# A decode kernel with attention and a gated MLP: wq loaded in two pieces of 16 and 112 partitions, and three small moves at the kernel's end

## The chip, the cores and the metric

One core of a Trainium2 chip. The time is the device time of one execution in microseconds, the median of several runs; lower is better. The fast runs of one kernel lie within 0.2% of each other here. The profile is of one execution, and its own span is about 2 us shorter than the time (656.2 us for a run of 658.23).

## The reference, cut to what matters

```python
x = A_x                                            # (2, 1, 512), bf16
h = x + attention(layernorm(x), k_cache, v_cache, wq, wo)   # 32 heads of 128, 8192 cached positions
h2 = h + (relu(ln_h @ W_gate) * (ln_h @ W_up)) @ W_down     # ln_h = layernorm(h), F = 1376
```

Two rows of input meet 2 x 128 MB of key and value cache. The weights add 4 MB each for wq and wo and 4.2 MB for the MLP. All of it is read once, 281 MB in total.

## The kernel before

Each engine has its own list of instructions with explicit semaphores (a helper called `s`). SP issues the loads. VectorE multiplies keys by queries and adds them up. TensorE does the rest of the sums. The parts that matter here:

```python
wq_v = vt.rearrange("p t d -> p (t d)")[:, 0:KC * Hq * Dh].rearrange("p (c n) -> p c n", c=KC)
s.dma("sp", "dwq", lambda: sync.dma_start(
    out=wq_v, in_=A_wq.rearrange("(p c) n -> p c n", p=P)), writes=["va", "vb", "vc"])
load_k(0, 0, T // 2)          # keys, 4 MB
load_k(0, T // 2, T)
load_k(1)                     # 8 MB
# ... cut: norm of x, q from wq, then 16 rounds over groups of heads ...
```

wq goes into the buffer that later holds values. Each of the 128 partitions gets one contiguous row of 32 KB. The first value load waits until q is computed.

The end of the kernel, shortened:

```python
s.op("pe", lambda: mlp_in(0, gate_ps, 0, KC), reads=["hd", "gate"], ...)   # gate
# ... variance of h; up, whose last part waits for its own load; then the PE jumps ...
s.op("pe", lambda: y_rows(eye_of[:, 0:B], ar, first=True), ...)   # the residual rows into y
# ... VectorE jumps, then act = gate * up; ScalarE jumps, then act_t = columns of act ...
# ... y += act_t @ W_down, whose four slices have a load each (wda, wdb, wdc, wdd) ...
# ... y to SBUF, two stores (SP and ACT), GpSimd waits for both, then clears all semaphores ...
```

"Jumps" are branches. The code of PE, VectorE and ScalarE is laid out in parts that a small loop takes in turn, and each engine branches once to its last part.

The softmax here doesn't subtract the row's maximum and nothing guards it: scores larger than these inputs give would overflow.

Of the kernel before, what the change touches and what calls it, by code (L numbers as in the profile page):

```python
# [13 lines left out]
def _view(t, offset, dims):  # L14
    return bass.AP(tensor=t.tensor, offset=t.offset + offset, ap=[t.ap[0]] + list(dims))
# [89 lines left out]
def kernel(  # L105
# [13 lines left out]
    nc = tc.nc  # L119
    P = nc.NUM_PARTITIONS  # L120
    B, Sq, D = A_x.shape
    _, Hkv, Sk, Dh = A_k_cache.shape
    Hq = A_wq.shape[1] // Dh
    F = B_W_gate.shape[1]
    KC = D // P
# [39 lines left out]
    def sbuf(name, shape, dtype):  # L165
        return nc.alloc_sbuf_tensor(name, shape, dtype).ap()
# [8 lines left out]
    om = sbuf("om", (P, TG * Dh), f32)  # L175
# [10 lines left out]
    eye_of = sbuf("eye_of", (P, Q), f32)  # L186
# [20 lines left out]
    hd = sc2[0][:, P // 2:P].bitcast(bf16).rearrange("p (c k b) -> p c k b", k=NR, b=B)  # L207
    r2 = late[:, 2 * NK - 1:2 * NK]
    x_late = wl[0:B, NK * D + 4 * P:NK * D + 4 * P + D]
    act_t = late[:, 2 * NK:2 * NK + FC * B // 2].bitcast(bf16).rearrange("p (f b) -> p f b", b=B)  # L210
# [7 lines left out]
    y_ps = psum("y", (P, D // 2))  # L218
    sm_ps = psum("sm", (P, 512))

    s = Streams(nc, ("pe", "dve", "act", "pool", "sp"))
    for name in ("v_in", "v_two", "p_in", "p_two", "o_in", "half", "q0", "q1", "z_in", "z_out"):
        s.sem(name)
    pe, dve, act, pool, sync = nc.tensor, nc.vector, nc.scalar, nc.gpsimd, nc.sync
# [4 lines left out]
    for name, value in (("v_two", 16 * (NLOOP - 1)), ("p_two", NLOOP), ("o_in", 1), ("q0", 1),  # L229
# [6 lines left out]
        out=ident, in_=ident, compare_op=ALU.not_equal, fill=1.0, base=0, pattern=[[-1, P]],  # L236
# [9 lines left out]
    for h in range(G):  # L246
        q = slice(h * Q, (h + 1) * Q)
        s.op("pool", lambda q=q: pool.tensor_copy(eye_of[q], ident[q, q]), reads=["ident"],
             writes=["eye"])
# [29 lines left out]
    def load_k(n, lo=0, hi=T):  # L279
        t = kt[n % 2]  # L280
        keys = [f"k{n % 2}{x}" for x in parts(lo, hi)]
        s.dma("sp", f"dk{n}_{lo}", lambda: sync.dma_start(
            out=t[:, lo:hi, :], in_=rows_of(A_k_cache, n)[:, lo:hi, :]), writes=keys)

    def load_v(n, lo=0, hi=T):
# [5 lines left out]
    wq_v = vt.rearrange("p t d -> p (t d)")[:, 0:KC * Hq * Dh].rearrange("p (c n) -> p c n", c=KC)  # L291
    s.dma("act", "dx", lambda: act.dma_start(out=x_row, in_=A_x.rearrange("b s d -> (b s) d")),
          writes=["x_row"])
    s.dma("sp", "dwq", lambda: sync.dma_start(  # L294
        out=wq_v, in_=A_wq.rearrange("(p c) n -> p c n", p=P)), writes=["va", "vb", "vc"])
    load_k(0, 0, T // 2)
    load_k(0, T // 2, T)
    load_k(1)
# [4 lines left out]
         reads=["eps"], writes=["warm"])  # L303
# [9 lines left out]
    def columns_of_x():  # L313
        for c in range(KC):
# [8 lines left out]
         reads=["hs", "mean"], writes=["st"])  # L323
    s.op("dve", lambda: dve.tensor_tensor(
        out=xd, in0=xc, in1=mu_ps.unsqueeze(1).to_broadcast([P, KC, B]), op=ALU.subtract),
        reads=["xc", "st"], writes=["xd"])
    s.op("pool", lambda: pool.tensor_tensor(out=sq, in0=xd, in1=xd, op=ALU.mult), reads=["xd"],
         writes=["sq"])
    reduce_c(sq, ["sq"])
    s.op("pe", lambda: pe.matmul(out=var_ps, lhsT=mean_f, rhs=hs, start=True, stop=True),  # L330
         reads=["hs", "mean"], writes=["st"])
    s.op("act", lambda: act.activation(out=rstd, in_=var_ps, func=ACT.Sqrt, bias=eps_t, scale=1.0),
         reads=["st", "eps"], writes=["rstd"])
    s.op("dve", lambda: dve.reciprocal(out=rstd, in_=rstd), reads=["rstd"], writes=["rstd"])
    s.op("pool", lambda: pool.tensor_tensor(
        out=xnb, in0=_view(xd, 0, [[B, KC], [1, B], [0, Q]]),
        in1=_view(rstd, 0, [[0, KC], [1, B], [0, Q]]), op=ALU.mult), reads=["xd", "rstd"],
        writes=["xnb"])
    s.op("act", lambda: act.activation(out=warm, in_=xnb[0:1, 0, 0, 0:1], func=ACT.Exp),
         reads=["xnb"], writes=["warm"])  # L340
# [21 lines left out]
    for r in range(NR2):  # L362
        i, h = divmod(r, G)
        for b in range(B):
# [4 lines left out]
            if b and r < NR2 - 1:  # L369
                s.op("act", fn, writes=[key], extra=extra, gives=(f"q{r % 2}", 1),  # L370
                     token=("act", s.count["act"] + 1))
# [148 lines left out]
    for k, lo, hi in WO:  # L520
        r0 = k * NS * G * Dh
        s.dma("sp", f"dwo{k}_{lo}", lambda k=k, lo=lo, hi=hi, r0=r0: sync.dma_start(
            out=wo_sb[:, k * JG + lo:k * JG + hi, :].rearrange("p k n -> p (k n)"),
            in_=A_wo[r0:r0 + NS * G * Dh, :].rearrange("(p j) n -> p j n", p=P)[:, lo:hi, :]
            .rearrange("p j n -> p (j n)")),
            writes=[f"wo{k}_{lo}"], extra=w_free)

    s.dma("act", "dx2", lambda: act.dma_start(out=x_late, in_=A_x.rearrange("b s d -> (b s) d")),
          writes=["x_late"], extra=w_free)
# [15 lines left out]
    for key, g, w, c0, c1 in (("gate", 0, B_W_gate, 0, KC), ("up0", 1, B_W_up, 0, KC - 1),  # L545
                              ("up1", 1, B_W_up, KC - 1, KC)):
        s.dma("sp", "d" + key, lambda g=g, w=w, c0=c0, c1=c1: sync.dma_start(  # L547
            out=wgu[:, g, c0:c1].rearrange("p c n -> p (c n)"),
            in_=w.rearrange("(p c) n -> p (c n)", c=KC)[:, c0 * F:c1 * F]),
            writes=[key], extra=x_free)  # L550
# [7 lines left out]
    def load_down(key, f0, r0, rows, r):  # L558
# [12 lines left out]
        out=zs, in0=zb.rearrange("p (g u) -> p g u", u=NS),  # L571
        in1=_view(head_blk, 0, [[0, B * NGR], [1, NS]]), op=ALU.mult), reads=["head"],
        writes=["zs"], extra=[("z_out", NGR * B)])
    red(zi, zs, AXIS.X, ["zs"], ["zi"])
    s.op("dve", lambda: dve.reciprocal(out=zi, in_=zi), reads=["zi"], writes=["zi"])
    for k in range(NGR):
        if k == NGR - 1:
            gather(B * NGR - 1)
        s.op("dve", lambda k=k: dve.tensor_tensor(
            out=oc[:, k * JG:(k + 1) * JG, :], in0=ou[:, :, k].rearrange("p b j -> p j b"),  # L580
            in1=_view(zi, k, [[0, JG], [NGR, B]]), op=ALU.mult),
            reads=[f"ou{b * NGR + k}" for b in range(B)] + ["zi"], writes=[f"oc{k}"])
# [17 lines left out]
    for k, lo, hi in WO:  # L600
# [7 lines left out]
        out=ht, in_=ar_ps.rearrange("p (q i c) -> p c q i", i=Q, c=KC)),  # L608
        reads=["mm0"], writes=["osb0", "osb1", "osb2", "osb3", "mm0"])
    ar = om  # L610
    s.op("act", lambda: act.activation(out=ar, in_=ar_ps, func=ACT.Copy), reads=["mm0"],
         writes=["om"])
# [3 lines left out]
    def columns_of_h():  # L616
        for q in range(P // Q):
# [6 lines left out]
         reads=["hs", "mean"], writes=["st"])  # L624
# [3 lines left out]
        out=hd, in0=_view(hc, 0, [[B, KC], [0, NR], [1, B]]),  # L628
        in1=_view(mu_ps, 0, [[0, KC], [0, NR], [1, B]]), op=ALU.subtract), reads=["xc", "st"],
        writes=["hd"])  # L630
    s.op("dve", lambda: dve.tensor_tensor(
        out=xd, in0=hc, in1=mu_ps.unsqueeze(1).to_broadcast([P, KC, B]), op=ALU.subtract),
        reads=["xc", "st"], writes=["xd"])
    s.op("dve", lambda: dve.tensor_tensor(out=sq, in0=xd, in1=xd, op=ALU.mult), reads=["xd"],
         writes=["sq"])
    red(ss, _view(sq, 0, [[0, FT * NR], [1, B], [B, KC]]), AXIS.X, ["sq"], ["ss"])

    def y_rows(lhsT, rhs, first=False, last=False):
        m = lhsT.shape[1]
        for c in range(2):  # L640
            end = pe.matmul(out=y_ps[c * 2 * Q:c * 2 * Q + m], lhsT=lhsT,  # L641
                            rhs=rhs[:, c * D // 2:(c + 1) * D // 2],
                            start=first, stop=last, skip_group_check=True)
        return end

    up_ps = mm_ps[1]

    def mlp_in(g, ps, c0, c1):
        for c in range(c0, c1):
            for j in range(FT):  # L650
                last = pe.matmul(out=ps[j * Q:(j + 1) * Q, 0:NM],
                                 lhsT=hd[:, c].rearrange("p a b -> p (a b)"),
                                 rhs=wgu[:, g, c, j:F:FT],
                                 start=(c == 0), stop=(c == KC - 1), skip_group_check=True)
        return last

    s.op("pe", lambda: mlp_in(0, gate_ps, 0, KC), reads=["hd", "gate"], writes=["gate_o"])
    var_col = st_ps[:, 32:33]
    s.op("pe", lambda: pe.matmul(out=var_col, lhsT=ss.rearrange("p a b -> p (a b)"), rhs=mean_c,
# [4 lines left out]
    s.op("dve", lambda: dve.tensor_scalar(  # L664
        out=gt, in0=gate_ps[:, 0:NM], scalar1=0.0, scalar2=r2, op0=ALU.max, op1=ALU.mult),
        reads=["gate_o", "r2"], writes=["osb0", "osb1", "osb2", "osb3"])
    up_mostly = s.op("pe", lambda: mlp_in(1, up_ps, 0, KC - 1), reads=["hd", "up0"],
                     writes=["mm1"])
    s.wait("pe", [s.last["up1"]])
    s.op("pe", lambda: mlp_in(1, up_ps, KC - 1, KC), reads=["hd", "up1"], writes=["mm1"])  # L670
    s.cut("pe")
    s.op("pe", lambda: y_rows(eye_of[:, 0:B], ar, first=True), reads=["eye", "om"], writes=["y"])
    s.op("dve", lambda: dve.tensor_tensor(
        out=gn.rearrange("p (q j) -> p q j", j=FT), in0=_view(gt, 2 * P, [[1, NQR], [0, FT]]),
        in1=_view(head_blk, 0, [[0, NQR], [1, FT]]), op=ALU.mult),
        reads=["osb0", "head"], writes=["gn"])
    s.wait("dve", [up_mostly])
    s.cut("dve")
    s.op("dve", lambda: dve.tensor_tensor(out=actr, in0=gt[:, 0:2 * P], in1=up_ps[:, 0:2 * P],
                                          op=ALU.mult), reads=["osb0", "mm1"], writes=["act"])  # L680
    s.op("dve", lambda: dve.tensor_tensor(
        out=actn[:, 0:FR].rearrange("p (q j) -> p q j", j=FT),
        in0=gn.rearrange("p (q j) -> p q j", j=FT), in1=_view(up_ps, 2 * P, [[1, NQR], [0, FT]]),
        op=ALU.mult), reads=["gn", "mm1"], writes=["act_n"])

    act_ps = sm_ps[:, 32:32 + FA * B].rearrange("p (f b) -> p f b", b=B)
    actn_ps = rep_ps[:, 32:32 + 3 * B].rearrange("p (f b) -> p f b", b=B)
# [8 lines left out]
    def columns_of_rest():  # L696
        for u in range(3):
# [4 lines left out]

    s.op("pe", columns_of_act, reads=["act", "ident"], writes=["sm"])
    s.op("pe", columns_of_rest, reads=["act_n", "row_b"], writes=["rep"])
    s.wait("act", [s.last["up1"]])
    s.cut("act")
    s.op("act", lambda: act.activation(out=act_t[:, 0:FA], in_=act_ps, func=ACT.Copy),
         reads=["sm"], writes=["act_t"])
    s.op("dve", lambda: dve.tensor_copy(act_t[:, FA:], actn_ps), reads=["rep"], writes=["act_l"])

    def add_y(f0, f1):
# [4 lines left out]
    for key, act_key, f0, f1 in (("wda", "act_t", 0, FT), ("wdb", "act_t", FT, FA),  # L716
                                 ("wdc", "act_l", FA, FC - 1), ("wdd", "act_l", FC - 1, FC)):
        s.op("pe", lambda f0=f0, f1=f1: add_y(f0, f1), reads=[act_key, key], writes=["y"])
    y_row = sc2[0][:, P:2 * P].bitcast(bf16)
# [1 line left out]
    s.op("dve", lambda: dve.tensor_copy(y_row[y0], y_ps[y0]), reads=["y"], writes=["y0"])  # L721
    s.op("act", lambda: act.activation(out=y_row[y1], in_=y_ps[y1], func=ACT.Copy), reads=["y"],
         writes=["y1"])
    ends = []
    for c, rows, eng, e in ((0, y0, "sp", sync), (1, y1, "act", act)):
        ends.append(s.dma(eng, f"dy{c}", lambda c=c, rows=rows, e=e: e.dma_start(
            out=out.rearrange("b s d -> (b s) d")[:, c * D // 2:(c + 1) * D // 2],
            in_=y_row[rows]), reads=[f"y{c}"]))
    sems = [h.num for h in s.sems.values()]
    s.wait("pool", ends)  # L730
    s.lists["pool"].append(((), lambda: pool.sem_clear(range(min(sems), max(sems) + 1)), None))



# [4 lines left out]

    engines = (("sp", sync), ("pool", pool), ("act", act), ("pe", pe), ("dve", dve))  # L740
    inner = nc.cur_bb
    for name, engine in engines:
        only = OrderedEngineSet([engine.engine])
        if name in s.cuts:
            nc.br(f"{name}_top", engines=only)
        else:
            s.emit(name, engine)
            nc.br("done", engines=only)
# [61 lines left out]
```

## Time and profile before

| | before |
|---|---|
| time | 658.23 us (658.0 to 658.88, 3 runs) |
| profiled span | 656.2 us |
| load queue busy, share of 16 engines | 99.3% |
| VectorE busy | 93% |
| last of wq landed | 13.39 us |
| last of W_down landed | 653.08 us |

The landings are the last of the sixteen semaphore increments that the trace has for each load of weights, keys or values.

### The profile page before, as it was taken

The numbers are of one execution on the slowest core, as the hardware profiler recorded it, in microseconds if no ns is written. First come the engines' busy times: TensorE is split into PE (matmuls) and PEld (weight loads), VectorE is DVE, ScalarE is ACT, GpSimd is POOL, SyncE is SP. The second block draws the span as 40 slices with busy tenths as digits, with TensorE's granted clock in tenths as the row PEclk, the third lists the DMA queues.
The fourth block names the chain that finished last, engine by engine and source line by source line (L and its number), as shares of the span: only waits on it lengthen the run. The fifth ranks groups of instructions, "written<-read, shape, count | busy, mean of one in ns | idle before, by whom it ended". The sixth has DMA issues, their size and how long they took to land.

```text
span 656.2 us, 3121 instructions
## 1 busy us (share of the span) xinstructions
PE 120.3 (18%) x1212; PEld 49.8 (8%) x1212; DVE 612.7 (93%) x172; ACT 63.2 (10%) x161; POOL 6.4 (1%) x27
## 2 busy tenths in 40 slices
PE   2400302103030110302003030300303030031256
PEld 1100101001010000101001010100101010010012
DVE  0699999999999999999999999999999999999973
ACT  2501001010101001010100101010010101001021
POOL 3000000000000000000000000000000000000000
PEclk9855755657565565756556575555657556565756
DMA  9999999999999999989999999989999999999997
GB/s 380 451 443 411 423 447 447 423 407 447 447 447 391 439 447 447 443 387 447 447 447 415 415 447 447 443 387 447 447 447 427 403 447 447 443 403 432 425 420 311
DMA packets 6613, 281.12 MB, mean 428 GB/s; under 512 B 744, under 2 KB 848, under 8 KB 1360
## 3 DMA queue, kind: packets, MB, share of 16 engines
q1 hardware_dynamic: 6596, 281.06, 99.3%
q8 instruction: 2, 0.03, 0.0%
q14 instruction: 3, 0.02, 0.0%
q10 hardware_dynamic: 12, 0.01, 0.0%
HBM read 281.06 MB, written 0.00 MB: 428 GB/s over the span
## 4 chain that ended last, share of the span: by engine, by line
DVE 75%; DMA 24%; issue 0%; SPq 0%; PE 0%
DVE k L386 34%; DVE k L391 33%; DMA k<-in_A_k_cache_dram 21%; DVE sc L243 4%; DMA k<-in_B_W_down_dram 3%; DVE osb L471 2%; DVE om L466 1%; SPq L547 0%; DVE ou L243 0%; SPq L559 0%; DVE rep L478 0%; PE y L641 0%; DVE sc L721 0%; SPq L294 0%; SPq L805 0%
## 5 line engine op out<-in xcount | busy, mean ns | idle before, releaser
L386 DVE TENSOR_TENSOR k<-k,qrep 128x32768 bf16<-128x32768 bf16 (+3 forms) x18 | 275.8, 15322 | 6.2 <-DMA k<-in_A_k_cache_dram 6.1
L391 DVE TENSOR_TENSOR k<-k 128x8192 bf16<-128x8192 bf16 (+4 forms) x69 | 266.9, 3868 | 2.4
L417 PE MATMUL o<-v,pm 128*32 128x512 bf16 x1024 | 93.8, 544 | 478.8 <-PEq L432 478.8
L404 ACT ACTIVATE pm<-sc 32x256 bf16<-32x256 f32 (+2 forms) x68 | 48.0, 705 | 560.1 <-DVE sc L243 559.3
L417 PEld LDWEIGHTS o<-v,pm 128*32 128x32 bf16 x1024 | 38.5, 130 | 533.5 <-issue 527.7
L243 DVE TENSOR_REDUCE sc<-k 128x256 f32<-128x2048 bf16 (+2 forms) x17 | 36.6, 2151 | 0.1
L471 DVE TENSOR_REDUCE osb<-om 128x128 f32<-128x512 f32 x16 | 16.3, 1018 | 0.6
L404 ACT ACTIVATION_READ_ACCUMULATOR pm<-sc 32x1 f32 x68 | 15.7, 231 | 0.0
L466 DVE TENSOR_TENSOR om<-o,turn_of 128x512 f32<-128x512 f32 x16 | 10.9, 682 | 3.9 <-PE o L417 3.9
L350 PE MATMUL mm<-v,om 128*64 x32 | 9.5, 432 | 6.6 <-PEq L348 6.6
L243 DVE TENSOR_REDUCE pick<-ident 128x8 f32<-128x128 bf16 x1 | 0.4, 382 | 10.7 <-ACT qrep L367 10.7
L367 ACT ACTIVATE qrep<-mm 32x512 bf16<-32x512 f32 x16 | 9.4, 587 | 6.1 <-PE mm L350 5.2
L451 PE MATMUL rep<-osb,spread 128*32 128x128 f32 x32 | 2.6, 421 | 37.1 <-DVE osb L471 37.1
L538 POOL TENSOR_TENSOR zm<-zm,zx 128x1 f32<-128x1 f32 x1 | 0.2, 192 | 625.9 <-PE o L417 625.9
L320 DVE COPY xc<-st 128x8 f32<-128x8 f32 x1 | 0.2, 167 | 6.5 <-PE st L315 6.5
L350 PEld LDWEIGHTS mm<-v,om 128*64 128x64 bf16 x32 | 3.9, 121 | 11.8 <-issue 11.0
L607 DVE STREAM_TRANSPOSE osb<-mm 128x512 f32<-128x512 f32 x1 | 0.7, 716 | 3.8 <-PE mm L593 3.8
L593 PE MATMUL mm<-k 128*2 128x512 bf16 x32 | 3.8, 621 | 0.3 <-DMA k<-in_A_wo_dram 0.3
L451 PEld LDWEIGHTS rep<-osb,spread 128*32 128x32 f32 x32 | 0.8, 140 | 37.5 <-DVE osb L471 37.5
L446 PE MATMUL sm<-zm,same 128*128 128x16 f32 x8 | 1.8, 297 | 0.4 <-PEq L432 0.4
L721 DVE CAST sc<-y 2x256 bf16<-2x256 f32 x1 | 0.4, 413 | 1.5 <-PE y L641 1.5
L240 POOL MEMSET pm<- 128x2048 bf16 x1 | 1.8, 1805 | 0.1
(81 smaller groups left out, 34.9 us busy)
## 6 DMA issues: line engine op xcount, KB each, us to landing
v<-in_A_v_cache_dram SPq DMA_DIRECT2D x4, 4096.0 KB, 20.3
k<-in_A_k_cache_dram SPq DMA_DIRECT2D x2, 4096.0 KB, 26.3
v<-in_A_wq_dram SPq DMA_DIRECT2D x1, 4096.0 KB, 12.4
k<-in_A_wo_dram SPq DMA_DIRECT2D x1, 2048.0 KB, 20.2
k<-in_A_wo_dram SPq DMA_DIRECT2D x2, 1024.0 KB, 23.2
k<-in_B_W_gate_dram SPq DMA_DIRECT2D x1, 1376.0 KB, 13.2
k<-in_B_W_up_dram SPq DMA_DIRECT2D x1, 1032.0 KB, 15.3
k<-in_B_W_down_dram SPq DMA_DIRECT2D x2, 512.0 KB, 17.0
```

The costliest lines, as they stand in the source:

```text
L240: s.op("pool", lambda: pool.memset(pm, 0.0), writes=["pm"])
L243: s.op("dve", lambda: dve.tensor_reduce(out=out_, in_=in_, axis=axis, op=ALU.add), reads=reads, writes=writes)
L350: last = pe.matmul(out=mm_ps[t][0:B * Q], lhsT=xnb[:, c].rearrange("p b q -> p (b q)"), rhs=wq_r[:, c, :, bass.ds(r * 2 + t, 1), :], start ...
L367: fn = lambda src=src, dst=dst: act.activation(out=dst, in_=src, func=ACT.Copy)
L386: s.op("dve", lambda: dve.tensor_tensor(out=kp, in0=kp, in1=_view(qrep[:, b, i, :], 0, [[0, hi - lo], [1, Dh]]), op=ALU.mult), reads=keys ...
L391: s.op("dve", lambda half=half, width=width: dve.tensor_tensor(out=kp[:, :, 0:half], in0=kp[:, :, 0:half], in1=kp[:, :, half:width], op=AL ...
L404: last = act.activation(out=p_of[ps, lo // TG:hi // TG, :, h], in_=sc2[n % 2][ps, lo:hi].rearrange("p (g t) -> p g t", t=TG), func=ACT.Exp ...
L417: last = pe.matmul(out=o_ps[g:g + W2], lhsT=pm[:, t // TG, :], rhs=vt[:, t:t + TG, :].rearrange("p t d -> p (t d)"), start=(t < P // Q * T ...
L451: last = pe.matmul(out=rep_ps[u * Q:(u + 1) * Q, :], lhsT=spread.rearrange("k h m -> k (h m)"), rhs=osb[:, u, :], start=True, stop=True, s ...
L466: s.op("dve", lambda: dve.tensor_tensor(out=om.rearrange("p (t d) -> p t d", d=Dh), in0=o_ps.rearrange("p (t d) -> p t d", d=Dh), in1=_vie ...
L471: s.op("dve", lambda: dve.tensor_reduce(out=osb[:, n % NS, :], in_=om.rearrange("p (t d) -> p d t", d=Dh), axis=AXIS.X, op=ALU.add), reads ...
L593: last = pe.matmul(out=ar_ps[g:g + B], lhsT=oc[:, k, :], rhs=wo_sb[:, k, :], start=False, stop=(k + P // Q >= NK), skip_group_check=True)
```

## The change

Its intent, as far as the code tells: get work out of the last microseconds, and get the first load going in a small piece. There are four parts.

```diff
-    s.dma("sp", "dwq", lambda: sync.dma_start(
-        out=wq_v, in_=A_wq.rearrange("(p c) n -> p c n", p=P)), writes=["va", "vb", "vc"])
+    for lo, hi in ((0, P // 8), (P // 8, P)):
+        s.op("sp", lambda lo=lo, hi=hi: sync.dma_start(
+            out=wq_v[lo:hi], in_=A_wq.rearrange("(p c) n -> p c n", p=P)[lo:hi]),
+            writes=["va", "vb", "vc"], gives=("dwq", 16), token=("dwq", 16 if lo == 0 else 32))
...
+    s.op("pe", lambda: y_rows(eye_of[:, 0:B], ar, first=True), reads=["eye", "om"], writes=["y"])
     s.op("pe", lambda: mlp_in(0, gate_ps, 0, KC), reads=["hd", "gate"], writes=["gate_o"])
...
     s.cut("pe")
-    s.op("pe", lambda: y_rows(eye_of[:, 0:B], ar, first=True), reads=["eye", "om"], writes=["y"])
...
-    s.wait("dve", [up_mostly])
-    s.cut("dve")
     s.op("dve", lambda: dve.tensor_tensor(out=actr, in0=gt[:, 0:2 * P], in1=up_ps[:, 0:2 * P],
...
+    s.wait("dve", [s.last["act"]])
+    s.cut("dve")
...
-    s.wait("act", [s.last["up1"]])
-    s.cut("act")
     s.op("act", lambda: act.activation(out=act_t[:, 0:FA], in_=act_ps, func=ACT.Copy),
          reads=["sm"], writes=["act_t"])
+    s.wait("act", [s.last["act_t"]])
+    s.cut("act")
...
-    s.wait("pool", ends)
-    s.lists["pool"].append(((), lambda: pool.sem_clear(range(min(sems), max(sems) + 1)), None))
+    s.wait("pool", [("gone", 2)])                 # both stores issued
+    s.lists["pool"].append(((), clear, None))     # all semaphores but y_out
+    s.lists["pool"].append(
+        ((), lambda: pool.wait_ge(s.sem("y_out"), 32).then_inc(s.sem("y_out"), -32), None))
```

More of the change, by code (lines that the diff above doesn't have):

```diff
@@ L219, with clear @@
     sm_ps = psum("sm", (P, 512))
-    s = Streams(nc, ("pe", "dve", "act", "pool", "sp"))
+    s = Streams(nc, ("y_out", "pe", "dve", "act", "pool", "sp"))
+    def clear():
+        sems = [h.num for k, h in s.sems.items() if k != "y_out"]
+        pool.sem_clear(range(min(sems), max(sems) + 1))
     for name in ("v_in", "v_two", "p_in", "p_two", "o_in", "half", "q0", "q1", "z_in", "z_out"):
@@ L293 @@
           writes=["x_row"])
-    s.dma("sp", "dwq", lambda: sync.dma_start(
-        out=wq_v, in_=A_wq.rearrange("(p c) n -> p c n", p=P)), writes=["va", "vb", "vc"])
+    for lo, hi in ((0, P // 8), (P // 8, P)):
+        s.op("sp", lambda lo=lo, hi=hi: sync.dma_start(
+            out=wq_v[lo:hi], in_=A_wq.rearrange("(p c) n -> p c n", p=P)[lo:hi]),
+            writes=["va", "vb", "vc"], gives=("dwq", 16), token=("dwq", 16 if lo == 0 else 32))
+        for k in ("va", "vb", "vc"):
+            token = s.last.pop(k)
+    for k in ("va", "vb", "vc"):
+        s.last[k] = token
     load_k(0, 0, T // 2)
@@ L666 @@
         reads=["gate_o", "r2"], writes=["osb0", "osb1", "osb2", "osb3"])
-    up_mostly = s.op("pe", lambda: mlp_in(1, up_ps, 0, KC - 1), reads=["hd", "up0"],
-                     writes=["mm1"])
+    s.op("pe", lambda: mlp_in(1, up_ps, 0, KC - 1), reads=["hd", "up0"], writes=["mm1"])
     s.wait("pe", [s.last["up1"]])
@@ L723 @@
          writes=["y1"])
-    ends = []
     for c, rows, eng, e in ((0, y0, "sp", sync), (1, y1, "act", act)):
-        ends.append(s.dma(eng, f"dy{c}", lambda c=c, rows=rows, e=e: e.dma_start(
+        s.op(eng, lambda c=c, rows=rows, e=e: e.dma_start(
             out=out.rearrange("b s d -> (b s) d")[:, c * D // 2:(c + 1) * D // 2],
-            in_=y_row[rows]), reads=[f"y{c}"]))
-    sems = [h.num for h in s.sems.values()]
-    s.wait("pool", ends)
-    s.lists["pool"].append(((), lambda: pool.sem_clear(range(min(sems), max(sems) + 1)), None))
+            in_=y_row[rows]), reads=[f"y{c}"], gives=("y_out", 16))
+        s.lists[eng].append(((), lambda e=e: e.sem_inc(s.sem("gone"), 1), None))
+    s.wait("pool", [("gone", 2)])
+    s.lists["pool"].append(((), clear, None))
+    s.lists["pool"].append(
+        ((), lambda: pool.wait_ge(s.sem("y_out"), 32).then_inc(s.sem("y_out"), -32), None))
     engines = (("sp", sync), ("pool", pool), ("act", act), ("pe", pe), ("dve", dve))
     inner = nc.cur_bb
+    for name in [w for ops in s.lists.values() for waits, _, gives in ops
+                 for w in [k for k, _ in waits] + ([gives[0]] if gives else [])]:
+        s.sem(name)
     for name, engine in engines:
```

## The prediction

The forecast's sum came to 659.0 us (657.0 to 665.0). It stands between rival (a), in which the split of wq costs nothing (657.9), and rival (b), in which the places that the two pieces are written to slow them (661 to 666, centred at 662.5). The chance for slower by 2% (above 671.4 us) was 0.025. The "hint" is one for (b): packets that slow each other.

> **What bounds the kernel now.** I read the page from the top: busy shares, slices, queues, chain. First the shares, the DMA row and the queue:
>
> ```profile
> span 656.2 us, 3121 instructions
> ...
> PE 120.3 (18%) x1212; PEld 49.8 (8%) x1212; DVE 612.7 (93%) x172; ACT 63.2 (10%) x161; POOL 6.4 (1%) x27
> ...
> DMA  9999999999999999989999999989999999999997
> GB/s 380 451 443 411 423 447 447 423 407 447 447 447 391 439 447 447 443 387 447 447 447 415 415 447 447 443 387 447 447 447 427 403 447 447 443 403 432 425 420 311
> ...
> q1 hardware_dynamic: 6596, 281.06, 99.3%
> ```
>
> Two resources are nearly full: VectorE at 93% and the one load queue at 99.3% of sixteen engines. The queue wins. The packet records of the trace have the first load packet at 1.97 us and the last at 652.60 us, and in each 10 us between there is at most 0.01 us without sixteen packets in flight. A 64 KB packet takes 2.42 us, so sixteen engines move 16 x 65,536 B / 2.42 us = 433 GB/s, and 281.06 MB at that rate takes 649 us. That is the span less the 2 us ahead of the first packet and the roughly 4 us after the last. VectorE is not the bound: its step of one group of heads takes 37.75 us (in the chain its products start at 97.45 and at 135.19 us), but key loads land 38.7 us apart (90.87, 129.58 and 168.29 us), so it catches up and from 400 us on waits for keys, as the chain in order of time shows:
>
> ```profile
> 398.29 2.20 DVE sc L243
> 400.51 38.69 DMA k<-in_A_k_cache_dram
> 439.22 17.24 DVE k L386
> ```
>
> The stretch the change edits is the end. The chain there:
>
> ```profile
> 635.21 17.67 DMA k<-in_B_W_down_dram
> 652.88 0.14 issue
> 653.02 0.51 PE y L641 x6
> 653.53 0.02 issue
> 653.55 0.41 DVE sc L721
> ```
>
> and from the timeline, VectorE's jump, ScalarE's table load, the residual rows and the stores:
>
> ```profile
> 650.23 1.28 ACT L707 ACT_TABLE_LOAD   x1 [4.91 <-DMA k<-in_B_W_up_dram]
> ...
> 650.39 1.02 PE L641 MATMUL y<-om,eye_of 128*2 128x256 f32 x4 [0.30 <-issue]
> 650.69 0.42 DVE L679 TENSOR_TENSOR qrep<-osb,mm 128x256 bf16<-128x256 f32 x1 [0.92 <-PE mm L651]
> ...
> 653.96 0.27 ACTq L726 DMA_DIRECT2D out_dram<-sc  x1
> 653.99 0.31 SPq L726 DMA_DIRECT2D out_dram<-sc  x1
> ```
>
> The reader should see that the end is released by the last slices of W_down. Their landings, from the semaphore increments of the trace: first slice 650.83, second 652.14, third 652.88, fourth 653.08 us. The work that the change hurries stands in front of the first slice only.
>
> At the other end, the start:
>
> ```profile
> 0.95 0.39 SPq L294 DMA_DIRECT2D v<-in_A_wq_dram  x1
> ...
> 13.99 3.21 PE L350 MATMUL mm<-v,om 128*64 x8 [5.11 <-PEq L348]
> ...
> 23.13 8.69 DVE L386 TENSOR_TENSOR k<-k,qrep 128x16384 bf16<-128x16384 bf16 x1 [2.31 <-DMA k<-in_A_k_cache_dram]
> ```
>
> Here the sixteen first packets, 32 KB each, start between 1.97 and 2.78 us and take 1.23 to 2.51 us; every later one of that size takes 1.21. This stagger never heals: wq's sixteen semaphore increments come over 12.65 to 13.39 us, and those of a key load at 594 us over 593.44 to 594.03. So what each engine loses in the first 4 us it still lacks at the end, and the slowest engine sets the time.
>
> [...] The trace agrees for 128 and 96 partitions: sixteen increments each. [...] One hint: while the last 96-partition slice overlapped the third slice, late 2 KB packets took 95, 114 and 122 ns against 84 to 91 for nearly all others, and late 1 KB packets 60 to 74 ns against 46; but most of the overlapping ones were not slowed, so I count it as weak. [...] In the trace ScalarE's jump costs 0.66 us, from the landing it waited for (649.57) to the table load (650.23).
>
> **The change, part by part.**
> *Residual rows ahead of the gate.* Four fp32 matmuls, 1.02 us busy, leave the stretch at 650.39, where they held the PE until about 651.3 and the columns of act to 651.34. They now start when ScalarE's copy of the rows ends (644.72 + 0.60 = 645.32) and the mean matmul is through (645.58). Gate could start at 646.25, so it slips by at most 645.58 + 1.02 - 646.25 = 0.35 us; but up waits for its DMA until 648.68, while gate and the variance matmul would end near 648.2 to 648.5 instead of 648.2. Path cost: 0.
> *VectorE's and ScalarE's jumps.* Up ends at 650.11 by its semaphore; the product that needs it began at 650.69, after the jump. Without a jump in between it starts near 650.13: 0.56 us earlier. With PE free too, the columns start at about 650.6 and ScalarE, its table load no longer ahead of it, has act ready near 650.9, not 651.79. ScalarE's table load moves behind: 650.9 + 0.66 + 1.28 = 652.85, still ahead of y at 653.55, a margin of 0.7 us. VectorE's jump falls beside the product of 0.51 us and two short matmul groups. So the first slice's matmuls start at about 651.35 instead of 651.83. But the second slice lands at 652.14, the third at 652.88, the fourth at 653.08, and eight matmuls take about 0.6 us: 652.14 + 0.6 = 652.75 is before the third landing. The half microsecond ends in a wait for W_down. Path gain: 0 to 0.05 us.
> *One wait for both stores.* In the trace the last store lands at 655.24, then GpSimd clears the semaphores (117 ns) and the closing handshake follows. The clear now runs once both stores are issued, at about 654.3, beside the 0.9 us of the store. Left behind is one wait with a decrement, an instruction of 17 ns. Gain: 117 - 17 = 0.10 us, perhaps 0.05 more of dispatch.
> *wq in two pieces.* One more issue of about 0.4 us on SP, with the DMA engines already busy: free. The bytes are equal. What counts is when the slowest engine has its share, and that reaches the end in full, as shown above.
>
> **The rivals for wq.**
> (a) [...] The small first piece may get the engines going more evenly. The most it can recover is the stagger, 0.7 us between first and last engine, of which a half if all became equal to the mean; it may also do nothing. Shift -0.5 to +0.2 us, then with the tail -0.15: about 657.9. For it: nearly unslowed 1 KB packets in the 96-partition slice, and the remainder of the change, which looks for tenths of a microsecond.
> (b) [...] Time: 661 to 666. [...]
> (c) *A new wait at the end.* If the later table load took y's place on the path, or the gate's slip delayed up. Margins of 0.7 and about 0.2 us: at most some +0.3 us.
>
> **Range and chances.** I give (a), with or without (c), 0.6 and (b) 0.4. (a) centres at 657.9, (b) at 662.5. I place the number between, nearer to (a): 659.0. The low end, 657.0, is the best of (a): 658.23 - 0.15 - 0.5 less the run-to-run 0.4, rounded to 657.0. The high end, 665.0, holds most of (b). Faster by 2% would need 645 us, below the 649 us of the loads alone: 0.005. [...]
>
> **What would show it.** First wq packets at 1.2 to 1.9 us mean (a)[...]; wq's landing near 13.4 or beyond 16 us says the same, and each later key landing must be shifted by the same amount as the end. Act should be ready near 650.9 plus that shift, PE should then wait for W_down's second slice, and the store's landing should be followed by about 0.1 us less than before. I am wrong if the end moves and wq's landing does not, if the start's shift is absorbed by 600 us, or if the chain's end is no longer W_down.

## More of the kernel before

The prediction shows the main lines. Two more views are needed later. First the page's list of DMA issues, with KB and microseconds from issue to landing:

```profile
v<-in_A_wq_dram SPq DMA_DIRECT2D x1, 4096.0 KB, 12.4
```

Second, the view by windows: start and end, length, busy time of PE, its weight loads, VectorE, ScalarE and GpSimd with instruction counts, clock, DMA share, GB/s.

```profile
4.00:14.00 10.00, 1.48 (x9) 1.23 (x9) 1.13 (x7) 1.75 (x3) 3.21 (x14) 1.00 1.03 446
14.00:24.00 10.00, 8.52 (x29) 3.51 (x29) 1.25 (x2) 7.36 (x13) 0.00 (x0) 1.00 0.99 426
```

The reader should keep the last two columns: the DMA engines are fully occupied (shares of 1.03 and 0.99), and they move 426 to 446 GB/s from the start. The view counts a packet whole in the stretch in which it starts, so the share can pass 1, and stretches of a few microseconds are rough.

## The result, and the profile after

| | before | after |
|---|---|---|
| time | 658.41 us (658.0 to 658.88, 4 runs) | 666.91 us (666.74 to 667.03, 4 runs) |
| profiled span | 656.2 us | 665.0 us |
| last of wq landed | 13.39 us | 22.54 us |
| a key load near the end landed | 594.03 us | 603.13 us |
| last of W_down landed | 653.08 us | 662.00 us |

The changed kernel is 1.3% slower: ratio 1.0129, 95% interval 1.0111 to 1.0146. Ratios here are the mean time of one kernel's fast runs over that of the other's fast runs of the same rounds, so they are not quite the ratio of the quoted medians. Each set of experiments had its own runs of the kernel before; "over the kernel before" is against their median (658.16 to 658.46 us).

The page after: span, DMA rows, queue, and the issue line of wq's larger piece.

```profile
span 665.0 us, 3124 instructions
...
DMA  9999999999999999999999999999999999999997
GB/s 213 367 430 441 441 441 438 438 438 398 434 441 441 441 438 438 430 406 434 441 441 441 438 438 426 406 438 441 441 441 438 438 426 406 438 441 428 426 419 310
...
q1 hardware_dynamic: 6612, 281.06, 99.2%
...
v<-in_A_wq_dram SPq DMA_DIRECT2D x1, 3584.0 KB, 21.2
```

The engines are as busy as before, 99.2% against 99.3%, and yet the first slice moved 213 GB/s instead of 380. The busy share does not tell the fast transfer from the slow one here. The same windows as before show it in figures:

```profile
4.00:14.00 10.00, 1.46 (x8) 1.21 (x8) 1.12 (x7) 1.75 (x3) 3.20 (x14) 1.00 0.88 210
14.00:24.00 10.00, 0.86 (x3) 0.42 (x4) 0.00 (x0) 0.00 (x0) 0.00 (x0) 1.00 1.03 308
```

And the timeline at the start: the first use of wq on the PE and the first products on VectorE.

```profile
23.14 4.82 PE L361 MATMUL mm<-v,om 128*64 x12 [12.59 <-PEq L359]
...
32.29 8.69 DVE L397 TENSOR_TENSOR k<-k,qrep 128x16384 bf16<-128x16384 bf16 x1 [1.92 <-DMA k<-in_A_k_cache_dram]
```

Both are 9.2 us later than before (13.99 and 23.13 us). The shift is made here, and the landings in the table carry it to the end. The chain at the end has the same form as before:

```profile
644.31 17.45 DMA k<-in_B_W_down_dram
661.76 0.14 issue
661.90 0.51 PE y L652 x6
662.41 0.02 issue
662.43 0.41 DVE sc L731
```

The trace also records each DMA packet. Here are the mean durations in us of the packets of 32 KB, taken in groups of sixteen in order of start, so about one row for each of the 16 engines. The ninth group belongs to the keys.

```
row      1     2     3     4     5     6     7     8   sum of 8    9
before  1.91  1.22  1.21  1.21  1.21  1.21  1.21  1.21   10.40   1.21
after   3.57  2.93  2.17  1.80  1.79  1.97  2.18  2.11   18.53   1.70
```

The difference of the sums is 8.13 us, and the ninth row adds 0.48 (1.697 - 1.213). That makes 8.6 us per engine, against 8.50 us between the medians. The whole loss lies in wq's rows and the first row behind them.

### The profile page after: what moved, and what is told of

The parts are those of the page before. It is cut to its first block, busy times and chain, and to the rows that moved or that the text cites. A ratio compares the mean times of both kernels' runs of the same rounds, so it can differ in the third digit from the quotient of the medians.

```text
span 665.0 us, 3124 instructions
## 1 busy us (share of the span) xinstructions
PE 118.5 (18%) x1212; PEld 49.2 (7%) x1212; DVE 612.6 (92%) x172; ACT 63.2 (10%) x161; POOL 6.4 (1%) x27
## 3 DMA queue, kind: packets, MB, share of 16 engines
q1 hardware_dynamic: 6612, 281.06, 99.2%
## 4 chain that ended last, share of the span: by engine, by line
DVE 74%; DMA 25%; SPq 0%; issue 0%; PE 0%
DVE k L397 34%; DVE k L402 33%; DMA k<-in_A_k_cache_dram 22%; DVE sc L248 4%; DMA k<-in_B_W_down_dram 3%; DVE osb L482 2%; DVE om L477 1%; SPq L558 0%; DVE ou L248 0%; SPq L570 0%; SPq L300 0%; DVE rep L489 0%; PE y L652 0%; DVE sc L731 0%; SPq L819 0%
## 5 line engine op out<-in xcount | busy, mean ns | idle before, releaser
L428 PE MATMUL o<-v,pm 128*32 128x512 bf16 x1024 | 92.3, 537 | 480.0 <-PEq L443 480.0
L378 ACT ACTIVATE qrep<-mm 32x512 bf16<-32x512 f32 x16 | 9.4, 586 | 14.0 <-PE mm L361 13.7
L652 PE MATMUL y<-k 128*2 128x256 bf16 x22 | 1.7, 271 | 0.5 <-DMA k<-in_B_W_down_dram 0.3
```

The lines of the kernel that those rows point to most:

```text
L378: fn = lambda src=src, dst=dst: act.activation(out=dst, in_=src, func=ACT.Copy)
L428: last = pe.matmul(out=o_ps[g:g + W2], lhsT=pm[:, t // TG, :], rhs=vt[:, t:t + TG, :].rearrange("p t d -> p (t d)"), start=(t < P // Q * T ...
```

## The experiments

Four theories stood. (1) Destinations: the partitions that the rows in flight together are written to set their pace. (2) Source addresses: the sixteen rows of the first piece lie side by side in HBM. (3) Seven rows per engine (112 over 16), an odd number, suit the load machinery badly. (4) Two loads that count on one semaphore are the cost.

In the first seven runs, figures that follow a cut directly are theory 1's.

### wq whole again

```diff
-    for lo, hi in ((0, P // 8), (P // 8, P)):  ...
+    s.dma("sp", "dwq", lambda: sync.dma_start(out=wq_v, in_=...), writes=["va", "vb", "vc"])
```

> The changed kernel with wq loaded in one piece again; residual rows, jumps and store wait stay. If the split of wq is the whole cause of the +8.5 us, the time is 658.1 to 658.5 us (658.41 before, less about 0.1 us for the store wait), wq's last increment is back at 13.4 us. If the moves at the end cost anything, it stays above 659 us.

Measured: 658.37 us (657.9 to 658.57) beside 658.46 for the kernel before; ratio 0.9999, interval 0.9986 to 1.0013. wq landed at 13.13 us. So the other three parts together are worth nothing that can be measured. The timeline of this run's end shows why:

```profile
650.82 0.60 PE L646 MATMUL y<-k 128*2 128x256 bf16 x8
...
651.34 1.28 ACT L726 ACT_TABLE_LOAD   x1 [0.69 <-ACT k L709]
651.75 0.31 PEld L646 LDWEIGHTS y<-k 128*2 128x2 bf16 x8 [0.63 <-DMA k<-in_B_W_down_dram]
...
653.17 0.08 PEld L646 LDWEIGHTS y<-k 128*2 128x2 bf16 x2 [0.31 <-DMA k<-in_B_W_down_dram]
```

In the kernel before, the same instruction is this one:

```profile
651.83 1.04 PE L641 MATMUL y<-k 128*2 128x256 bf16 x16
```

The first slice of W_down is now multiplied at 650.82 instead of 651.83 us. Of this 1.0 us, 0.4 are not the change's: in this execution the last piece of W_up had landed at 649.15 instead of 649.55 us. The gain that is left, 0.6 us, ends in two waits for W_down's next slices (the "<-DMA" in the brackets), and the last one starts at 653.17 us whatever came before (W_down's last landing is 653.13 us, before 653.08). ScalarE's table load fits in beside them. The store wait shows as 0.92 us from the last store's landing to the end of the span instead of 0.98, a gain of 0.06 us.

### The split of wq alone

```diff
 # the kernel before, with
+    for lo, hi in ((0, P // 8), (P // 8, P)):  ...
```

> The kernel before with wq in 16 and 112 partitions, nothing else changed. If the split is the whole cause: 666.8 to 667.2 us and wq landed near 22.5 us. If the loss needs one of the other parts, it is nearer to 658.4 us.

Measured: 667.35 us (667.02 to 668.09), ratio 1.0138 (1.0122 to 1.0153), last of wq at 22.84 us. The split alone makes the whole loss, 8.9 us here.

### Halves of 64 partitions

```diff
-    for lo, hi in ((0, P // 8), (P // 8, P)):
+    for lo, hi in ((0, P // 2), (P // 2, P)):
```

> The changed kernel with wq in 64 and 64 partitions. [...] 8 rows at 2 x 1.21 us = 19.4 us and +8 to +10 us over the kernel before. Source addresses (theory 2): [...] within 1 us of the kernel before. Odd number of rows per engine (theory 3): four rows each, so within 1 us. Two loads on one semaphore (theory 4): +8.5 us as in the changed kernel.

Measured: 668.75 us, ratio 1.0158 (1.0143 to 1.0174), 10.3 us over the kernel before, a little more than the 8 to 10 expected. The windows:

```profile
4.00:14.00 10.00, 0.58 (x2) 0.50 (x2) 0.71 (x5) 1.75 (x3) 3.22 (x14) 1.00 1.01 210
14.00:24.00 10.00, 0.00 (x0) 0.00 (x0) 0.00 (x0) 0.00 (x0) 0.00 (x0) 1.00 0.97 223
```

Half the rate for as long as wq lasts: 210 and 223 GB/s instead of 446 and 426. Nearly every row took 2.4 to 2.6 us, twice 1.21 and a little. Half of the partitions as destinations, half the rate: that is what theory 1 expected, though by a sharing that is not shown. Theories 2 and 3 expected no loss here. Theory 3 falls as the main cause. (What seven rows per engine cost by themselves, no run shows.) What theory 2 said of this run rested on an assumption about which rows are read at the same moment, so it is tested below.

### Two pieces along the row

```diff
+    for lo, hi in ((0, 1), (1, KC)):           # of the KC = 4 parts of each row
+            out=wq_v[:, lo:hi], in_=A_wq.rearrange("(p c) n -> p c n", p=P)[:, lo:hi]),
```

> The changed kernel with wq in two loads again, but cut along the row: 8 KB and 24 KB of each of all 128 partitions. [...] 658.0 to 658.8 us. Source addresses: 658 to 659 us. Two loads on one semaphore: near 667 us.

Measured: 658.13 us (657.77 to 658.62), ratio 0.9999 (0.9983 to 1.0014). Two loads on one semaphore cost nothing here. Theory 4 falls.

### The same places filled from elsewhere

```diff
-            out=wq_v[lo:hi], in_=A_wq.rearrange("(p c) n -> p c n", p=P)[lo:hi]),
+            out=wq_v[lo:hi], in_=<rows of the key cache, 64 KB apart>[lo:hi, ...]),
```

> The changed kernel, wq's two loads reading their 32 KB rows from the key cache at a step of 64 KB instead of from wq at a step of 32 KB; same destinations, wrong result on purpose. [...] the time stays at 666.5 to 667.5 us and wq's place is filled near 22.5 us. Source addresses: the first rows and the 112 change their pace, and the time moves by more than 1.5 us.

Measured: 667.25 us, ratio 1.0138 (1.0121 to 1.0155), place filled at 22.51 us, mean rows 3.68, 2.83, 2.15, 1.78, 1.84, 1.98, 2.12, 2.09 us, almost those of the changed kernel. (The query is wrong here; the comparison with the reference still passed, so its tolerance does not see it.) With other source addresses and the same destinations the loss is the same. Theory 2 falls.

### The first piece by itself

```diff
 # the kernel before, with, ahead of wq:
+    s.dma("sp", "dxtra", lambda: sync.dma_start(out=wq_x[0:16], in_=<16 rows of 32 KB>), ...)
```

`wq_x` is an unused place in the value buffer; the first value load waits for it too.

> The kernel before plus one extra load of 16 rows of 32 KB to partitions 0 to 15 ahead of wq, whose data nobody uses. If bytes were all, +1.2 us (one row per engine at 1.21 us): 659.7 us. [...] rows take 3.7 us as in the changed kernel, then eight rows at 1.21 in place of one at 1.9 and seven at 1.21: +3.0 us, 661.4 us.

Measured: 662.29 us, ratio 1.0064 (1.0047 to 1.0081), 4.13 us over the kernel before. Bytes alone are 1.21 us, so the destinations cost 2.9 us. The rows took 3.62 us, as expected, but the next row still took 2.19 us instead of 1.21. These 0.98 us in the row behind are what the expectation missed (0.9 us). Why part of the loss shows up there was not tested. The whole, 4.1 us, is what the estimate gives if these sixteen rows move at a quarter of the undisturbed rate: 4 x 1.21 us for them and 1.21 for the next, less the 1.91 that the first row takes in the kernel before.

### The same rows, at a step of eight partitions

```diff
-        out=wq_x[0:16], ...
+        out=wq_x[0:P:8], ...
```

> As the run before, same sixteen source rows, but to partitions 0, 8, 16 to 120[...]. [...] rows of 2.4 to 2.6 us, +1.8 us, 660.2 us, between bytes alone (659.7) and the sixteen neighbouring partitions (661.4). Source addresses: the same as the run before.

Measured: 660.18 us, ratio 1.0033 (1.0017 to 1.005), with rows of 2.01 us and then 1.67. Same bytes, same source, other destinations: 2.1 us less, and the two sets of runs do not overlap (660.13 to 660.70 against 662.10 to 662.76). The expected time was met; the rows were shorter than the 2.4 to 2.6 us expected, and the row behind was longer, as in the run before.

### The second piece by itself

```diff
+    s.dma("sp", "dxtra", lambda: sync.dma_start(out=wq_x[16:P], in_=<112 rows of 32 KB>), ...)
```

> The kernel before plus an extra load of 112 rows to partitions 16 to 127 ahead of wq, unused. Bytes alone: seven rows per engine, +8.5 us, 666.9 us. If the 112 are slow by themselves, as in the changed kernel where they took 14 to 15 us: +14 us, 672 to 673 us. If they were slow there only because the first 16 left the engines out of step: near 667.

Measured: 672.45 us, ratio 1.0219 (1.0202 to 1.0236), 14.3 us over the kernel before. Bytes alone are 8.5, so the destinations cost 5.8 us. With the 2.9 us of the first piece that makes 8.7, against 8.5 to 8.9 measured for the split. The two pieces add up.

Why 112 rows lose this much is not shown; the author's estimate rested on an assumed sharing and is cut. The trace shows how the loss is spread. All packets of the load queue together took 13.7 us more per engine than in the kernel before, so the mean loss over the bytes is 5.2 us, near the 5.8 in the time. And the engines stay together: the sixteen increments of a key load near 600 us lie within 1.3 us (606.92 to 608.23; before, 0.6). So the loss falls on all engines, not on a late few.

Six small runs look for the reason. Each puts a few unused rows of 24 KB behind wq, so that their packets can be told from those of 32 KB; undisturbed, a 24 KB row takes 0.91 us. Most of their times are near the noise, and the packets carry the reading. Which engine takes which row is not in the trace. With sixteen packets in flight, n small rows leave 16 - n to the key load; these are "the others" below. A "pair" is two rows whose places lie 32 partitions apart.

### Eight rows at a step of four, from partition 0

```diff
+    s.dma("sp", "dxtra", lambda: sync.dma_start(out=wq_x[0:32:4], in_=<8 rows of 24 KB>), ...)
```

> The kernel before plus, behind wq, an unused load of eight 24 KB rows to partitions 0, 4 to 28[...]. Any theory: the eight packets take 0.91 us (24/32 of 1.21), eight engines lose that much, the time is +0.9 us, 659.1 us.

Measured: eight packets of 0.912 us, all 32 KB packets at 1.21; 659.23 us, ratio 1.0012 (0.9995 to 1.0029).

### Eight rows at a step of four, from partition 4

```diff
+        out=wq_x[4:36:4], ...
```

> The same rows to partitions 4, 8 to 32[...]. [...] 0.91 us a packet but for short overlaps with a neighbour that is not through with wq, up to 1.2 us. If [...]: 1.4 us or more a packet.

Measured: again eight packets of 0.912 us; of the rows around them three took 1.24 to 1.46 us; 659.78 us, ratio 1.0024 (1.0007 to 1.004). The packets themselves are as undisturbed from partition 4 as from partition 0. The rival that expected 1.4 us or more falls.

### Eight rows at a step of eight, in pairs

```diff
+        out=wq_x[0:64:8], ...
```

The question was whether packets of another load, written beside these, are held up.

> The same rows to partitions 0, 8 to 56[...]. Sharing: 1.8 us a packet, +1.8 us, 660.0 us. [...] the 32 KB packets of the key load on the other eight engines, 1.21 us otherwise, are longer at that moment; if not, they stay at 1.21.

Measured: 660.34 us, ratio 1.003 (1.0014 to 1.0047). The eight packets took 1.20 to 1.50 us, less than the 1.8 expected, and the eight 32 KB key packets that began beside them took 1.91 to 2.07 us instead of 1.21. The windows of the run at a step of four from partition 0, then of this one:

```profile
12.60:14.60 2.00, 0.71 (x2) 0.41 (x3) 0.00 (x0) 0.00 (x0) 0.00 (x0) 1.00 0.99 426
```

```profile
12.60:14.60 2.00, 0.38 (x1) 0.24 (x2) 0.00 (x0) 0.00 (x0) 0.00 (x0) 1.00 1.11 324
```

The last column is rough in so short a window (the kernel before has 344 there). With the bytes of each packet spread evenly over its duration, these 2 us hold 432 GB/s at a step of four and 284 here. Eight rows in pairs slow themselves and the rows of another load beside them; eight rows at a step of four did neither.

### One pair, partitions 0 and 32

```diff
+        out=wq_x[0:64:32], in_=<2 rows of 24 KB>
```

> As the eight pairs, but only two rows of 24 KB, to partitions 0 and 32[...]. [...] (as the key rows of 1.5 to 2.1 us beside the eight pairs suggest), key rows of the other engines take longer than 1.21 us while these two packets run[...]. If only the two engines are held up, their packets take about 1.8 us, all other rows stay at 1.21, and the even slowness of the 112 rows stays unexplained. Time: +1 to +2 us in both cases, as the two engines set the end.

Measured: 659.45 us, ratio 1.0016 (0.9999 to 1.0032). The two packets took 1.16 and 1.22 us and the rows behind them 1.56 and 1.64; all other rows stayed at 1.21. One pair slowed only itself and the two rows behind it. (Packet and row behind together are 2.7 and 2.9 us, near the 1.8 + 1.2 expected, but split in another way.)

### Two pairs, and four neighbouring rows

```diff
+        out=wq_x[0:64:16], in_=<4 rows of 24 KB>     # two pairs: partitions 0, 16, 32, 48
```

```diff
+        out=wq_x[0:4], in_=<4 rows of 24 KB>         # four neighbours: partitions 0 to 3
```

Each expectation has two rivals: either the four rows are enough to stretch the others, or they are not.

> Four rows of 24 KB to partitions 0, 16, 32, 48[...]. One pair left all other engines' rows at 1.21 us, four pairs stretched all of them to 1.5 to 2.1 us. [...] some stretch of the others, 1.3 to 1.7 us. If two are still too few: others stay at 1.21, the four packets and the rows behind them take about 2.8 us together as with one pair.

> Four rows of 24 KB to partitions 0 to 3[...]. [...] the other twelve engines' rows are stretched above 1.3 us while the four run. [...] others stay at 1.21, and the four need 4 x 0.91 = 3.6 us for the rows in place of 0.91.

One look each, state unknown; the packets are compared within each trace. Two pairs: the others took 1.7 to 2.3 us (660.76 us). Four neighbouring rows: the others took 2.7 to 3.2 us, the longest of all (661.63 us), and the four packets 1.7 to 2.6. The window of this second run:

```profile
12.60:14.60 2.00, 0.00 (x0) 0.00 (x0) 0.00 (x0) 0.00 (x0) 0.00 (x0) 1.00 0.73 123
```

The 123 GB/s, too, count packets by their start; spread over their durations, the packets of these 2 us make 185 GB/s, against 432 with eight rows at a step of four. Four rows of 24 KB, to neighbouring partitions or in two pairs, were enough to slow the rows in flight with them, the neighbours most. The number of pairs counts as well: one pair slowed only itself and the rows behind it, two and four pairs also the others. In both runs the first rival stands, though the two pairs' stretch passed the 1.3 to 1.7 us expected, and the second falls.

What stays open: how the rows are dealt to the engines, since the trace names neither engine nor partition of a packet, and where on their way the packets hold each other up. That the 112 rows are slow because packets hold each other up fits the loss that falls on all engines; it is argued from the small runs, not shown in the 112-row load itself.

No version beats the kernel before beyond the noise. The two nearest, wq whole and wq cut along the row, have ratios of 0.9999 each.

## Why the prediction was wrong

It said 659.0 us, 657.0 to 665.0, and the time was 666.91. That the two kernels would lie within 2% was right. Point by point:

- **What bounds the kernel: right.** The last landing of wq came 9.15 us later, that of the key load near 600 us 9.10, that of W_down 8.92, and the time grew by 8.5. Almost nothing was absorbed. One reading was loose: in some 10 us (130 to 140 us) up to 0.18 us pass with fewer than sixteen packets in flight, not 0.01; the conclusion stands.
- **The residual rows and the jumps: right in effect.** With wq whole, the time did not move. Counted from the last landing of W_up (649.55 us before, 649.15 with wq whole), act was ready after 1.50 us (650.47 + 0.18 - 649.15; predicted 1.35) and the first slice started after 1.67 (predicted 1.80, before 2.28). The wait for W_down took all of the gain. Rival (c) did not come: in the changed kernel the table load ended at 662.04 us, 0.39 ahead of its use.
- **The store wait: right in sign, smaller.** 0.06 us instead of 0.10 to 0.15.
- **The steps that failed: the choice between (a) and (b), and the size of (b).** The text chose (a): "I give (a), with or without (c), 0.6 and (b) 0.4". The runs showed (b), and more of it than the text allowed. The first 16 rows cost 2.9 us over their bytes (the extra 16 rows alone). The 112 rows cost 5.2 us per engine in the mean and 5.8 in the time (the extra 112 alone). The terms that the text had for the two rested on figures from outside and on an assumed fair sharing. Its (b) centred at 662.5 us, 4.4 short of the time. The small runs, where rows to a few places also slow the rows beside them, fit a larger loss; in the 112-row load itself that is argued.
- **The range did not hold its own sum.** The prediction said that "the slowest engine sets the time" and gave (b) up to 666 us, but the upper end was put at 665.0, "most of (b)". Both are short of the 666.91 measured. In the changed kernel the sixteen increments of the key load near 600 us lie within 1.2 us (601.91 to 603.13), so all engines were late, not one.
- **The evidence was read with the wrong weight.** For (a) the text had two soft signs: that few packets of 1 KB in the 96-partition slice were slowed, and that the rest of the change "looks for tenths of a microsecond". The first is weak, as a pair alone lost only 0.6 and 0.7 us with the rows behind it (1.16 + 1.56 and 1.22 + 1.64 instead of 0.91 + 1.21 us) and left all other rows at 1.21. The second is a guess about intent and says nothing about the chip.

## What to carry to other kernels

Here the load queue was busy from the first packet to the last, and a delay at the start was paid almost in full at the end (9.15 us at wq's landing, 8.5 in the time), so in such a kernel look at the first packets' durations and not at the busy share. If a load must be cut, try it along its rows with all 128 partitions in every piece: here that cost nothing and gained nothing (ratio 0.9999). Pieces by partition cost 8.9 us (16 and 112, the split alone) and 10.3 us (64 and 64), and four rows to neighbouring partitions stretched the others from 1.21 us to between 2.7 and 3.2. Work taken off compute engines ahead of a transfer that ended later only lengthened the wait for that transfer: 0.6 us gained at the first slice of W_down, nothing in the time.
